# Second attention product with v as weights and the softmax moving, so that x comes out transposed

## The chip, the cores and the metric

One core of one Trainium2 chip. Times are device microseconds (us) of the whole program; lower is better. The kernel before takes 648.37 us (median of three runs, 646.69 to 648.68).

## What is computed

Chunked attention with 8 memory keys, then a SOLU layer with layer norm, then a mixture of 8 experts that sends each token to one expert. Only the first part is touched by the change:

```python
# q, k, v: (4, 8, 768, 64); mem_k, mem_v: (4, 8, 8, 64); chunk 32, left 16, right 8
for c in range(nc):                                  # 24 chunks of 32 queries
    k_full = concat([mem_k, k[:, :, l_start:r_end]]) # 8 + 56 keys
    v_full = concat([mem_v, v[:, :, l_start:r_end]])
    scores = q_c @ k_full.T / sqrt(64)
    a = exp(scores - max); a = a / (sum(a) + 1e-9)
    out[:, :, c_start:c_end] = a @ v_full            # the second attention product
x = out.transpose(0, 2, 1, 3).reshape(3072, 512)     # heads side by side
h = x @ w_in                                         # 512 -> 1024, then SOLU, layer norm, w_out
# ... then the experts
```

## The kernel before

The 3072 tokens go through in 24 row-tiles of 128 tokens, numbered i. A row-tile holds 4 chunks (`TC`) of 32 queries. Its 8 heads are 4 groups (`g`, `NG`) of 2 (`j`): j = 0 has its 64 keys on partitions 0 to 63, j = 1 on 64 to 127. `attention_steps` gives the steps of one row-tile (L352 to L458):

- `scores` (L357): 64 f32 matmuls of 64x32 weights into the PSUM tile `sc`.
- `row_max` to `normalise` (L372 to L405): the softmax, on VectorE, ScalarE and, for the last product, POOL.
- `transpose` (L407): four 128x128 transposes on PE into the PSUM tile `xb`, two banks, one buffer.
- `evacuate` (L414): ScalarE copies them to `aT` (keys on partitions, tokens along the row).
- `attend` (L419): the second product, 64 f32 matmuls. Weights are the softmax of one chunk and head (64 keys, 32 tokens), v moves (64 columns). Output: tokens on partitions, channels along the row, bank j.
- `x_hi`, `x_lo` (L433, L437): x times 256 as two f16 halves, the high one by ScalarE, the rest by VectorE (`low_half`, L185), into the tile `xhl` (two buffers). The profile puts `x_lo` at L186 with the names xhl<-xo.
- `x_turn` (L440): a transposing DMA from SP's queue turns `xhl` into `xT`, [channel, half and block of 128 channels, token], three buffers.

`product_in` of `solu_steps` (L526) takes `xT` as weights in 24 matmuls of 512 columns into the PSUM tile `h`, two banks and one buffer. `row_max`, `exp` and `times_h` (L543 to L559) read `h`; the next row-tile's product can only begin after `times_h`. Further down a row-tile comes `product_out` with w_out (24 matmuls, L607), `x2_hi`, `x2_lo`, `x2_turn`, and the routing.

The order on every engine is written out by hand. `at(t, fn)` notes a step with a planned time, and all of them are issued in order of t (L1363). From row-tile 7 on `steady(i)` gives the times (L460, `PERIOD` is 14.2); the first seven have tables (`STARTS`, `SOLU`, `CUTS`). An engine takes its instructions strictly in that order, so SP too: a DMA whose data isn't there holds up all DMAs behind it. SP issues the loads of q, k and v, of w_in and w_out (`load64`, L196), of the experts' weights, and the transposing DMAs of x, of the layer norm's output (`ln_turn`) and of x2.

In the first 70 us w_in and w_out, which come as 64-bit numbers, are turned into f16 halves by VectorE and ScalarE (`split64_steps`: L224, L229, L234, L241 and L186), beside the first row-tiles. `keep_warm` (L873) puts filling matmuls into PE's gaps there.

Near the end `other_slots` (L1088), in a branch that only runs when an expert gets far too many tokens, uses an `xhl` tile as scratch.

Of the kernel before, what the change touches and what calls it, by code (L numbers as in the profile page):

```python
# [8 lines left out]
F32 = mybir.dt.float32  # L9
F16 = mybir.dt.float16  # L10
# [9 lines left out]
P = 128  # L20
# [4 lines left out]
S_X = 2.0**8  # L25
# [13 lines left out]
def attention_solu_top1_moe(  # L39
# [145 lines left out]
    def low_half(lo, src, s, hi):  # L185
        nc.vector.scalar_tensor_tensor(out=lo, in0=src, scalar=s, in1=hi, op0=ALU.mult, op1=ALU.subtract)  # L186
# [165 lines left out]
    def attention_steps(i, s, a):  # L352

        u, tt, ib = i // 2, i % 2, i % TB
        v = {}

        def scores():  # L357
            qt, kt = QT[u], KT[u]
            sc = ps_s.tile([P, 2, HALF], F32, tag="s", name="sc")
            v["sc"] = sc[:, :, 0:NG * KW].rearrange("p j (g n) -> p j g n", g=NG)  # L360
            for g in range(NG):
                for c in range(TC):
                    for j in range(2):
                        nc.tensor.matmul(  # L364
                            out=v["sc"][CH * c:CH * (c + 1), j, g, :],
                            lhsT=qt[64 * j:64 * (j + 1), g, P * tt + CH * c:P * tt + CH * (c + 1)],
                            rhs=kt[64 * j:64 * (j + 1), g, TC * tt + c, :],
                            start=True,
                            stop=True,
                        )  # L370

        def row_max():  # L372
            if ib == 0:
                nc.vector.memset(v["sc"][0:CH, :, :, M:M + LEFT], MASKED)
            if ib == TB - 1:
                nc.vector.memset(v["sc"][P - CH:P, :, :, KW - RIGHT:KW], MASKED)
            v["mx"] = st.tile([P, 2, NG], F32, tag="mx", name="mx")
            nc.vector.tensor_reduce(out=v["mx"], in_=v["sc"], axis=AX.X, op=ALU.max)

        def shift():  # L380
            v["e"] = ap_.tile([P, NG, 2, KW], F32, tag="e", name="e")
            nc.vector.tensor_tensor(  # L382
                out=v["e"].rearrange("p g j n -> p j g n"),
                in0=v["sc"],
                in1=v["mx"].unsqueeze(3).to_broadcast([P, 2, NG, KW]),
                op=ALU.subtract,
            )

        def exp():
            nc.scalar.activation(out=v["e"], in_=v["e"], func=AF.Exp, scale=scale)  # L390

        def row_sum():
            v["sm"] = st.tile([P, NG, 2], F32, tag="sm", name="sm")
            nc.vector.tensor_reduce(out=v["sm"], in_=v["e"], axis=AX.X, op=ALU.add)

        def guard():
            nc.vector.tensor_scalar(out=v["sm"], in0=v["sm"], scalar1=1e-9, scalar2=None, op0=ALU.add)

        def recip():
            nc.vector.reciprocal(out=v["sm"], in_=v["sm"])  # L400

        def normalise():
            nc.gpsimd.tensor_tensor(  # L403
                out=v["e"], in0=v["e"], in1=v["sm"].unsqueeze(3).to_broadcast([P, NG, 2, KW]), op=ALU.mult
            )  # L405

        def transpose():  # L407

            v["xb"] = ps_x.tile([P, 2, HALF], F32, tag="x", name="xo")
            for g in range(NG):  # L410
                c = GD + g % 2 * P
                nc.tensor.transpose(v["xb"][:, g // 2, c:c + P], v["e"][:, g].rearrange("p j n -> p (j n)"), ident)

        def evacuate():  # L414
            v["aT"] = ap_.tile([P, NG, P], F32, tag="aT", name="aT")
            for z in range(2):
                nc.scalar.activation(out=flat(v["aT"][:, 2 * z:2 * z + 2]), in_=v["xb"][:, z, GD:GD + 2 * P], func=AF.Copy)

        def attend():  # L419
            aT, vv, xo = v["aT"], VW[u % 2], v["xb"]  # L420
            for g in range(NG):
                for c in range(TC):
                    for j in range(2):
                        nc.tensor.matmul(  # L424
                            out=xo[CH * c:CH * (c + 1), j, g * D:(g + 1) * D],
                            lhsT=aT[64 * j:64 * (j + 1), g, CH * c:CH * (c + 1)],
                            rhs=vv[64 * j:64 * (j + 1), TC * tt + c, g * D:(g + 1) * D],
                            start=True,
                            stop=True,
                        )  # L430
            v["xo"] = xo[:, :, 0:GD]

        def x_hi():  # L433
            v["xhl"] = lnp.tile([P, 2, 2, GD], F16, tag="xhl", name="xhl")
            nc.scalar.activation(out=v["xhl"][:, 0], in_=v["xo"], func=AF.Copy, scale=S_X)

        def x_lo():  # L437
            low_half(v["xhl"][:, 1], v["xo"], S_X, v["xhl"][:, 0])

        def x_turn():  # L440
            xT[i] = lnp.tile([P, 2 * KD, P], F16, tag="xT", name="xT", bufs=3)
            nc.sync.dma_start_transpose(out=xT[i], in_=v["xhl"].rearrange("p a j d -> p (a j d)"))

        steps = (row_max, shift, exp, row_sum, guard, recip, normalise)
        at(s[0], scores)
        if tt == 1 and u + 2 < NU and i > 3:
            if i > 5:
                at((i - 3) * PERIOD + 2.5, load_k, u + 2)
                at((i - 2) * PERIOD + 6.2, load_q, u + 2)
            at((i - 1) * PERIOD + 6.5, load_v, i + 3)  # L450
            at(i * PERIOD + 6.5, load_v, i + 4)
        for t, fn in zip(s[1:], steps):
            at(t, fn)
        for t, fn in zip(a, (transpose, evacuate, attend, x_hi, x_lo, x_turn)):
            at(t, fn)
        t = (i - 4) * PERIOD + 5.4
        at(WINDOWS.get(i, t), windows, i)
        at(MKEYS.get(i, t), memory_keys, i)  # L458
# [629 lines left out]
    def other_slots():  # L1088


        home = flat(lnp.tile([P, 2 * KD, P], F16, tag="x2T", name="x2T")).bitcast(F32)
        used = [0]

        def some_of(*shape):
            n = 1
            for x in shape:
                n *= x
            t, used[0] = home[:, used[0]:used[0] + n], used[0] + n
            return t.rearrange("p (a b) -> p a b", b=shape[1]) if len(shape) > 1 else t

        t1, cap, dl, be, em, es = (some_of(*x) for x in ((NT, E), (NT,), (NT,), (E,), (NO, E), (NO,)))
        oho = flat(lnp.tile([P, 2 * KD, P], F16, tag="x2T", name="x2T"))[:, 0:NT * NO].rearrange("p (a b) -> p a b", b=NO)
        keep_ = lnp.tile([P, 2, 2, GD], F16, tag="xhl", name="xhl").rearrange("p a j d -> p (a j d)").bitcast(F32)
        nc.vector.tensor_tensor(out=be, in0=rt["ends"], in1=rt["tr"], op=ALU.subtract)
        nc.vector.tensor_tensor(out=be, in0=be, in1=rt["room"][:, 2], op=ALU.subtract)
        for out_, of in ((cap, rt["room"][:, 0]), (dl, be)):
            nc.vector.tensor_tensor(out=t1, in0=oh_all, in1=of.unsqueeze(1).to_broadcast([P, NT, E]), op=ALU.mult)
            nc.vector.tensor_reduce(out=out_, in_=t1, axis=AX.X, op=ALU.add)
        nc.vector.tensor_tensor(out=cap, in0=rank_all, in1=cap, op=ALU.is_ge)
        nc.vector.tensor_tensor(out=dl, in0=rhi_all, in1=dl, op=ALU.add)  # L1110
        nc.vector.scalar_tensor_tensor(out=dl, in0=dl, scalar=1.0, in1=cap, op0=ALU.add, op1=ALU.mult)
        nc.vector.tensor_tensor(
            out=oho,
            in0=dl.unsqueeze(2).to_broadcast([P, NT, NO]),
            in1=iota_s[:, 1:NO + 1].unsqueeze(1).to_broadcast([P, NT, NO]),
            op=ALU.is_equal,
        )
        pt = ps_m.tile([P, 128], F32, tag="m", name="pm")
        ips = [pt[:, 0:NO], pt[:, 64:64 + NO]]
        for a in range(2):  # L1120
            three(ips[a], [(oav[:, i, a], oho[:, i]) for i in range(NT)])
        numbers("others", NO, ips, N - 1, keep_)
        nc.vector.tensor_tensor(
            out=em,
            in0=rt["ends"].unsqueeze(1).to_broadcast([P, NO, E]),
            in1=iota_s[:, 0:NO].unsqueeze(2).to_broadcast([P, NO, E]),
            op=ALU.is_le,
        )
        nc.vector.tensor_reduce(out=es, in_=em, axis=AX.X, op=ALU.add)
        nc.vector.tensor_scalar(out=rt["ctl"][:, 1, 0:NO], in0=es, scalar1=float(E - 1), scalar2=None, op0=ALU.min)  # L1130
# [367 lines left out]
```

## Time and profile before

| | |
|---|---|
| median of 3 runs | 648.37 us (646.69 to 648.68) |
| profiled execution | 647.3 us, span 645.6 us |
| mean granted PE clock | 0.987 |
| PE / VectorE / ScalarE / POOL busy | 607.8 / 419.3 / 299.1 / 176.5 us |
| DMA, all queues | 119.28 MB, mean 185 GB/s |

In the profile PE is TensorE's matmuls, PEld its weight loads, DVE VectorE, ACT ScalarE, POOL GpSimd and SP SyncE, which here only issues DMAs. L424 is line 424 of the kernel. Instructions are named output<-inputs: xo<-vw,aT is the second product. A matmul's recorded time includes its way through the array, so that many side by side overlap.

### The profile page before, as it was taken

The numbers are of one execution on the slowest core, as the hardware profiler recorded it, in microseconds if no ns is written. First come the engines' busy times: TensorE is split into PE (matmuls) and PEld (weight loads), VectorE is DVE, ScalarE is ACT, GpSimd is POOL, SyncE is SP. The second block draws the span as 40 slices with busy tenths as digits, with TensorE's granted clock in tenths as the row PEclk, the third lists the DMA queues.
The fourth block names the chain that finished last, engine by engine and source line by source line (L and its number), as shares of the span: only waits on it lengthen the run. The fifth ranks groups of instructions, "written<-read, shape, count | busy, mean of one in ns | idle before, by whom it ended". The sixth has DMA issues, their size and how long they took to land.

```text
span 645.6 us, 16935 instructions
## 1 busy us (share of the span) xinstructions
PE 607.8 (94%) x6919; PEld 333.3 (52%) x6919; DVE 419.3 (65%) x1216; ACT 299.1 (46%) x543; POOL 176.5 (27%) x201
## 2 busy tenths in 40 slices
PE   8787888999999999999999988999999999999993
PEld 4454344555545555555554443654554656657561
DVE  6999975878888788888786664447253435374020
ACT  5353644555556556565444223435243446354120
POOL 3122142323343324323334006022121313223101
PEclk9999898999999999999999989999999999999997
DMA  8899869989999999895539457988546576874201
GB/s 276 251 286 185 193 137 169 200 177 245 186 216 238 206 218 210 170 195 126 106 84 203 109 181 160 316 327 200 214 116 235 150 259 135 302 227 88 47 8 41
DMA packets 175654, 119.28 MB, mean 185 GB/s; under 512 B 133116, under 2 KB 157070, under 8 KB 175056
## 3 DMA queue, kind: packets, MB, share of 16 engines
q1 hardware_dynamic: 169488, 98.78, 64.7%
q0 software_dynamic: 6080, 19.34, 9.5%
q8 instruction: 56, 0.92, 0.6%
q14 instruction: 30, 0.25, 0.1%
HBM read 73.69 MB, written 12.94 MB: 134 GB/s over the span
## 4 chain that ended last, share of the span: by engine, by line
PE 31%; issue 26%; DVE 19%; DMA 11%; POOL 6%; ACT 5%; SPq 1%; POOLq 0%; ACTq 0%; DVEq 0%
PE pt L347 10%; PE h L535 10%; PE pg L347 5%; DMA out_dram<-eh,split 3%; POOL out_dram L1304 3%; POOL xg L1208 2%; DVE nm L545 2%; PE pt L1246 2%; DMA wd<-in_moe_w_in_dram 2%; ACT eh L553 2%; DVE eh L557 2%; PE xo L424 2%; DVE e L382 1%; PE sc L364 1%; DVE x L186 1%
## 5 line engine op out<-in xcount | busy, mean ns | idle before, releaser
L535 PE MATMUL h<-win_hl,xT 128*128 128x512 f16 x576 | 133.7, 383 | 6.2 <-DVE eh L557 1.9
L347 PE MATMUL pt<-wout_hl,lnT 128*128 128x512 f16 x552 | 129.5, 381 | 0.0
L1232 DVE SCALAR_TENSOR_TENSOR ru<-pg,ru 128x320 f16<-128x320 f32 (+5 forms) x72 | 37.7, 525 | 110.3 <-ACT ru L1231 110.3
L1246 PEld LDWEIGHTS <-ru 128*128 128x128 f16 (+2 forms) x1176 | 69.7, 100 | 62.2 <-issue 3.8
L535 PEld LDWEIGHTS <-xT 128*128 128x128 f16 x576 | 53.5, 98 | 67.5 <-issue 5.3
L347 PEld LDWEIGHTS <-lnT 128*128 128x128 f16 x576 | 53.6, 98 | 57.8 <-issue 1.4
L347 PE MATMUL pg<-xu,hl 128*128 128x320 f16 (+2 forms) x480 | 75.3, 317 | 2.6 <-DMA xu<-x 2.3
L1246 PE MATMUL pt<-hl,ru 128*128 128x512 f16 (+2 forms) x528 | 72.9, 321 | 0.0
L1231 ACT ACTIVATE ru<-pg 128x320 f16<-128x320 f32 (+5 forms) x72 | 33.5, 466 | 84.3 <-PE pg L347 83.2
L601 POOL TENSOR_TENSOR lnhl<-eh,lnhl 128x1024 f16<-128x1024 f32 x23 | 49.0, 2133 | 80.5 <-ACT lnhl L597 66.2
L347 PEld LDWEIGHTS <-hl 128*128 128x128 f16 x480 | 46.5, 99 | 27.9 <-DMA xu<-x 2.8
L1246 PE MATMUL pt<-wout_hl,ru 128*32 128x128 f16 (+2 forms) x648 | 59.9, 285 | 0.0
L347 PE MATMUL pg<-xu,win_hl 128*128 128x480 f16 (+3 forms) x384 | 59.3, 316 | 0.0
L1304 POOL DMA_INDIRECT out_dram<-eh,slots_sidx x17 | 17.6, 1037 | 144.3 <-ACT eh L1303 144.3
L347 PEld LDWEIGHTS <-win_hl 128*128 128x128 f16 x384 | 37.2, 98 | 21.3 <-issue 0.6
L553 ACT ACTIVATE eh<-h,nm 128x1024 f32<-128x1024 f32 x24 | 26.7, 1113 | 42.5 <-DVE zr L738 34.2
L186 DVE SCALAR_TENSOR_TENSOR hl<-wf,hl 128x1024 f16<-128x1024 f32 x32 | 38.6, 1223 | 6.4 <-ACT hl L1195 6.0
L403 POOL TENSOR_TENSOR e<-e,sm 128x512 f32<-128x512 f32 x24 | 26.7, 1114 | 49.3 <-ACT win_hl L241 20.2
L586 POOL TENSOR_TENSOR rt<-vr,mhalf 128x1 f32<-128x1 f32 x24 | 15.2, 633 | 79.1 <-DVE vr L582 79.0
L1195 ACT ACTIVATE hl<-wf 128x1024 f16<-128x1024 f32 x32 | 32.9, 1047 | 2.8 <-DMA wf<-in_moe_w_dram 2.8
L574 ACT ACTIVATE junk<-eh,su 128x1024 f16<-128x1024 f32 x24 | 27.5, 1148 | 13.9 <-DVE pr L569 9.8
L557 DVE SCALAR_TENSOR_TENSOR eh<-h,eh 128x1024 f32<-128x1024 f32 x24 | 29.3, 1221 | 4.9 <-ACT eh L553 4.8
(186 smaller groups left out, 825.3 us busy)
## 6 DMA issues: line engine op xcount, KB each, us to landing
wf<-in_moe_w_dram SPq DMA_DIRECT2D x14, 2048.0 KB
vw<-in_v_dram SPq DMA_DIRECT2D x96, 112.0 KB
kr<-in_k_dram SPq DMA_DIRECT2D x12, 560.0 KB
qt<-in_q_dram SPq DMA_DIRECT2D x12, 512.0 KB
x2d<-x POOLq DMA_DIRECT2D x23, 260.0 KB, 3.7
wd<-in_moe_w_in_dram SPq DMA_DIRECT2D x4, 1024.0 KB
wd<-in_moe_w_out_dram SPq DMA_DIRECT2D x4, 1024.0 KB
wf<-in_moe_w_dram SPq DMA_DIRECT2D x8, 512.0 KB
```

Of the source, the lines that this page charges most:

```text
L186: nc.vector.scalar_tensor_tensor(out=lo, in0=src, scalar=s, in1=hi, op0=ALU.mult, op1=ALU.subtract)
L347: nc.tensor.matmul(out=out_ap, lhsT=a, rhs=b_, start=(z == 0), stop=(z == n - 1))
L535: nc.tensor.matmul(out=v["h"][:, n * HALF:(n + 1) * HALF], lhsT=xt[:, a * KD + kk], rhs=win_hl[:, b_, kk, n * HALF:(n + 1) * HALF], start= ...
L553: nc.scalar.activation(out=v["e"], in_=v["h"], func=AF.Exp, bias=v["nm"], scale=IH, accum_out=v["se"])
L557: nc.vector.scalar_tensor_tensor(out=e, in0=v["h"], scalar=IH, in1=e, op0=ALU.mult, op1=ALU.mult, accum_out=v["su"])
L574: nc.scalar.activation(out=junk, in_=v["e"], func=AF.Square, bias=v["su"], scale=1.0, accum_out=v["sq"])
L601: eng.tensor_tensor(out=v["ln"][:, 1], in0=v["e"], in1=v["ln"][:, 0], op=ALU.subtract)
L1195: nc.scalar.activation(out=hl[b, m][:, 0, cs], in_=wf[m if of is None else of][:, cs], func=AF.Copy, scale=(S_W1, S_W2)[m])
L1231: nc.scalar.activation(out=r[:, 0, f, 0:cap(n)], in_=ps, func=AF.Relu)
L1232: nc.vector.scalar_tensor_tensor(out=r[:, 1, f, 0:cap(n)], in0=ps, scalar=0.0, in1=r[:, 0, f, 0:cap(n)], op0=ALU.max, op1=ALU.subtract)
L1246: nc.tensor.matmul(out=y_t[n, piece][q * m:(q + 1) * m, 0:DM // fold], lhsT=r[:, a, kk, at_:at_ + m], rhs=wt[:, b_, kk, q * DM // fold:(q ...
L1304: put = nc.gpsimd.indirect_dma_start(out=out if fold == 1 else out.rearrange("n (h d) -> (n h) d", h=fold), out_offset=bass.IndirectOffset ...
```

## The change

In `attend` the two operands trade places: the weights are v of one chunk and head (64 keys, 64 channels), and the softmax moves (32 tokens). The output has channels on partitions and tokens along the row: head h of a pair of groups g2 takes partitions 64h to 64h + 63, and bank j stays. With that `x_hi` and `x_lo` write `xT` itself, and `x_turn` and its DMA are taken out; `xT` is allocated in `x_hi`. The loops are turned so that matmuls in a row go to the four combinations of h and j. `xhl` is left with one buffer for the scratch of `other_slots`.

```diff
         def attend():
             aT, vv, xo = v["aT"], VW[u % 2], v["xb"]
-            for g in range(NG):
+            for g2 in range(NG // 2):
                 for c in range(TC):
-                    for j in range(2):
-                        nc.tensor.matmul(
-                            out=xo[CH * c:CH * (c + 1), j, g * D:(g + 1) * D],
-                            lhsT=aT[64 * j:64 * (j + 1), g, CH * c:CH * (c + 1)],
-                            rhs=vv[64 * j:64 * (j + 1), TC * tt + c, g * D:(g + 1) * D],
-                            start=True,
-                            stop=True,
-                        )
+                    t0_ = g2 * P + CH * c
+                    for h in range(2):
+                        g = 2 * g2 + h
+                        for j in range(2):
+                            nc.tensor.matmul(
+                                out=xo[D * h:D * (h + 1), j, t0_:t0_ + CH],
+                                lhsT=vv[64 * j:64 * (j + 1), TC * tt + c, g * D:(g + 1) * D],
+                                rhs=aT[64 * j:64 * (j + 1), g, CH * c:CH * (c + 1)],
+                                start=True,
+                                stop=True,
+                            )
             v["xo"] = xo[:, :, 0:GD]
 
         def x_hi():
-            v["xhl"] = lnp.tile([P, 2, 2, GD], F16, tag="xhl", name="xhl")
-            nc.scalar.activation(out=v["xhl"][:, 0], in_=v["xo"], func=AF.Copy, scale=S_X)
+            xT[i] = lnp.tile([P, 2 * KD, P], F16, tag="xT", name="xT", bufs=3)
+            v["xT"] = xT[i].rearrange("p (a j k) t -> p a j (k t)", a=2, j=2)
+            nc.scalar.activation(out=v["xT"][:, 0], in_=v["xo"], func=AF.Copy, scale=S_X)
 
         def x_lo():
-            low_half(v["xhl"][:, 1], v["xo"], S_X, v["xhl"][:, 0])
-
-        def x_turn():
-            xT[i] = lnp.tile([P, 2 * KD, P], F16, tag="xT", name="xT", bufs=3)
-            nc.sync.dma_start_transpose(out=xT[i], in_=v["xhl"].rearrange("p a j d -> p (a j d)"))
+            low_half(v["xT"][:, 1], v["xo"], S_X, v["xT"][:, 0])
...
-        for t, fn in zip(a, (transpose, evacuate, attend, x_hi, x_lo, x_turn)):
+        for t, fn in zip(a, (transpose, evacuate, attend, x_hi, x_lo)):
             at(t, fn)
...
-        keep_ = lnp.tile([P, 2, 2, GD], F16, tag="xhl", name="xhl").rearrange("p a j d -> p (a j d)").bitcast(F32)
+        keep_ = lnp.tile([P, 2, 2, GD], F16, tag="xhl", name="xhl", bufs=1).rearrange("p a j d -> p (a j d)").bitcast(F32)
```

## Rows read from the trace of the kernel before

**Rows 1.** The page: PE's busy share in 40 slices of the span, in tenths.
```profile
PE 607.8 (94%) x6919; PEld 333.3 (52%) x6919; DVE 419.3 (65%) x1216; ACT 299.1 (46%) x543; POOL 176.5 (27%) x201
...
PE   8787888999999999999999988999999999999993
```
**Rows 2.** Busy time by stretches (us): PE, PEld, DVE, ACT, POOL, clock, DMA share, GB/s.
```profile
20.00:68.60 48.60, 37.57 (x676) 21.17 (x675) 46.72 (x74) 21.64 (x39) 12.82 (x8) 1.00 0.87 228
...
100.00:340.00 240.00, 238.55 (x3482) 123.72 (x3463) 197.74 (x729) 134.24 (x271) 78.55 (x96) 0.99 0.88 182
```
**Rows 3.** PE's waits, 0 to 102 us: who waited for whom, total, times, longest.
```profile
PE h L535 <- DVE eh L557: 1.9, 1, 1.9
PE h L535 <- DMA xT<-xhl: 1.7, 1, 1.7
PE h L535 <- DVE win_hl L186: 1.4, 1, 1.4
```
**Rows 4.** PE's waits, 102 to 340 us.
```profile
PE xo L424 <- ACT aT L417: 0.3, 1, 0.3
PE sc L364 <- issue: 0.3, 1, 0.3
```
**Rows 5.** The chain of waits in order of time: start, us, what.
```profile
49.78 5.40 DMA wd<-in_moe_w_out_dram
...
68.69 6.95 PE h L535 x24
```
**Rows 6.** L224, 50 to 57 us: records' min/median/max (ns); timelines of VectorE and POOL.
```profile
L224 DVE TENSOR_SCALAR da<-wd x3: 684/1316/1317, 49.7 to 55.2; 128x1024 int32<-128x1024 int32 x3
...
53.75 2.77 DVE L224 TENSOR_SCALAR da<-wd 128x1024 int32<-128x1024 int32 x2
...
53.47 2.49 POOL L403 TENSOR_TENSOR e<-e,sm 128x512 f32<-128x512 f32 x2 [4.79 <-DVE su L566]
```
**Rows 7.** SP's timeline and its waits; tile xT: the turns' records, who waited.
```profile
49.78 0.58 SPq L203 DMA_DIRECT2D wd<-in_moe_w_out_dram  x1
...
SPq L442 <- DVE e L382: 8.8, 1, 8.8
...
L442 SPq DMA_TRANSPOSE xT<-xhl x24: 1231/1242/2407, 22.8 to 331.6; - x24
...
  PEld L535: 4.1, 3
```
**Rows 8.** PE's timeline in the steady stretch: start, us, what.
```profile
157.11 0.86 PE L424 MATMUL xo<-vw,aT 64*32 64x64 f32 x64
...
158.78 0.45 PE L347 MATMUL pm<-wg_hl,x2T 128*128 128x16 f16 x12
159.09 2.32 PE L535 MATMUL h<-win_hl,xT 128*128 128x512 f16 x10
```
**Rows 9.** Matmuls and weight loads by shape: records' min/median/max, or busy and mean.
```profile
L424 PE MATMUL xo<-vw,aT x1536: 212/217/313, 18.3 to 328.3; 64*32 64x64 f32 x192
...
L412 PE MATMUL xo<-ident,e x96: 272/273/329, 16.9 to 326.6; 128*128 128x128 f32 x96
...
L347 PEld LDWEIGHTS <-x2T x288: 94/96/98, 91.9 to 379.1; 128*128 128x128 f16 x144
...
L1246 PEld LDWEIGHTS <-ru 128*64 128x64 f16 x288 | 15.3, 110 | 2.5 <-issue 2.5
...
L1246 PEld LDWEIGHTS <-ru 128*32 128x32 f16 x384 | 5.4, 97 | 1.2 <-issue 1.2
```
**Rows 10.** x_hi in tile xhl's records: min/median/max (ns).
```profile
L435 ACT ACTIVATE xhl<-xo x24: 573/576/597, 19.3 to 330.3; 128x512 f16<-128x512 f32 x24
```
**Rows 11.** L424 alone, by stretches: length, PE busy (matmuls), PEld, clock, DMA, GB/s.
```profile
157.11:157.36 0.25, 0.25 (x32) 0.25 (x33) 1.00 1.51 441
...
99.69:100.06 0.37, 0.37 (x31) 0.37 (x33) 0.50 1.52 164
99.69:100.57 0.88, 0.88 (x64) 0.88 (x64) 0.50 1.28 205
```

## The prediction

> **What bounds the kernel now.** I read the busy line and the slices first [rows 1]: TensorE has work for 94% of the span, and its slices stand at 9 almost everywhere but in the first seven (some 113 us). So the question for every edit is whether it shortens TensorE's own queue, or one of the few places where that queue stands still. The table by stretches [rows 2] shows where these are. From 100 to 340 us, with attention and SOLU side by side, PE is busy for 238.55 of 240 us. From 20 to 68.6 us PE has gaps (37.57 of 48.60 us) and VectorE next to none (46.72). The list of PE's waits says the same from the other side: from 102 to 340 us two waits of 0.3 us are all that it lists [rows 4], and before that VectorE, on `times_h` or the halves of w_in, stands beside one wait of 1.7 us on the DMA of xT [rows 3]. The chain of waits [rows 5] crosses from VectorE to PE at 68.69 us, when the third row-tile's `times_h` frees the bank of h. From there on it mostly follows PE. An edit is thus worth something if it moves that crossing, or if it shortens PE's work after it.
>
> **The change part by part.**
> *The 24 transposing DMAs.* SP issues each in about 1.24 us [rows 7], 24 x 1.242 = 29.8 us of SP's queue, and the DMA engines lose their packets. In steady state neither is on the path: attention's x is ready well before its reader (`attend` is planned at (i-2) x PERIOD + 11, `product_in` at i x PERIOD), and PE lists no DMA wait from 102 to 340 us [rows 4]. I count nothing there. The cover is that distance, some 17 planned us, which the shorter way only lengthens.
>
> In the first 68 us the issue also held up whatever stood behind it on SP: for the third tile SP stood 8.8 us for x_lo, and the load of the last w_out quarter followed the turn at 49.78 [rows 7] and is the 5.40 us step of the chain [rows 5]. Without the turn the load can go that much earlier, as soon as its buffer is free. What is late next is VectorE itself: it did L224 of another quarter first, and the two together took 2.77 us, records of 1.316 and 1.317 where one alone has 0.684 [rows 6], so that 2.77 - 2 x 1.317 = 0.13 us was idle. Their excess lies beside two normalising operations on POOL (2.49 us from 53.47, until 55.96); no DMA is in it. So -0.1 us. The bounds: below, all VectorE idle time from 20 to 68.6 us, 48.60 - 46.72 = 1.9 us [rows 2]; above, the loads now crowd what they overtake, for which I allow 0.5. Other loads that were held behind the turns of tiles 0 and 1 feed the windows and scores, and VectorE, whose order is fixed, comes to these no sooner.
>
> PE's 1.7 us wait on xT (and the 4.1 of its weight loads) [rows 3, 7] is before the crossing too. The product that waits there next needs halves of w_in that VectorE is still splitting (the 1.4 us on win_hl in rows 3), so I count it at nothing; if that cover is gone it is inside the 1.9.
>
> *x_hi and x_lo.* Same shapes and engines, 0.58 us for x_hi [rows 10]; only the place written differs. They take xT's buffer (three deep) at x_hi instead of after x_lo. Its reader is the product of three tiles before, planned 26 us before x_hi, so ACT, in whose order the next row-tile's work stands behind x_hi, gains no wait. Nothing. The one allocation of xhl that is left belongs to a branch for overflowing experts, with no row in this trace: nothing.
>
> *The product itself.* 64 weight loads and 64 matmuls a tile before and after. A matmul now has 64 columns of v as weights and moves 32 instead of 64. Today 8 array tiles (two row halves, four column quarters) work side by side, then 4 (two halves, two halves). Stream time: a 128-column f32 matmul is recorded at 273 ns and a 64-column one at 217, so 64 columns are 56 ns [rows 9]. Shared by 8 tiles that is 7.0 ns a matmul; 32 columns are 28 ns, shared by 4 tiles 7.0 as well. No gain from the stream, but a shorter last one: 28 ns.
>
> The weight load doubles: f16 loads of 64 and 32 columns are recorded at 110 and 97 ns [rows 9], 13 ns for 32, so 27 ns for 64, no longer well under the stream of its tile but level with it. No row shows such a pair. Bounds: if the load stays under the stream, 7.0 ns a matmul. The nearest row where the load is the longer part is L347's logits, 12 matmuls of 16 columns from 158.78 to 159.09, 0.31/12 = 26 ns each [rows 8]. Its load is recorded at 96 ns and a 64-column one at 110 [rows 9], so 40 ns a tile, 10 a matmul over four.
>
> How much of that counts depends on what limits the product today. From its first to its last start it takes 0.86 - 0.22 = 0.64 us [rows 8, 9]. In the table for L424 alone [rows 11] the first 32 matmuls begin within 0.25 us, and the other 32 need the remaining 0.39. At the half clock (PEclk 0.50, the product at 99.69) the first 31 need 0.37 of 0.88 us and the rest 0.51, less apart. So at the full clock the array is not what holds the second half; the instructions come later than the array could take them, and their number stays. I charge the longer load to the first half alone: 32 x (0 to 3.0 ns) = 0 to 0.10 us, and take 0.05, the middle, since neither row is nearer. With the shorter last stream 0.05 - 0.028 = +0.02 us a tile. Products after the crossing without a longer wait behind them: tiles 6 to 23, 18 of them: +0.4 us, with bounds of 18 x -0.028 = -0.5 and 18 x 0.07 = +1.3.
>
> By the Trainium skill, "TensorE: Matmul & The Clock Gate", section "Packing small matmuls: row/col tiling", a weight load runs beside matmuls in flight only where its row group differs. By this rule the load would add to the stream of its own tile. The trace doesn't agree for today's shape: 32 matmuls in 0.25 us are under 8 ns each, where load and stream in turn would need (13 + 56)/8 = 8.6.
>
> *Sum.* -0.1 + 0.4 = +0.3 us. The profiled execution took 647.3 us (span 645.6 and 1.7 around it), within the three runs (646.69 to 648.68) and 1.07 under their median; I put the sum on the mean of the three, 647.9, which gives 648.2.
>
> **Rivals.**
> *The product gets longer (slower).* A 64x64 tile is held by one pair as long as a 64x32 tile is today, 53 to 56 ns, either because load and stream take turns (27 + 28) or because 32 columns take no less than 64. Four tiles then give 55/4 = 14 ns a matmul, 64 x 14 = 0.90 us for 0.64, less 0.03: +0.23 us on 18 tiles, +4.1, so 652.0. It decides once a pair holds its tile for more than about 40 ns (10 a matmul, today's mean). For it: no fp32 pair with a load as long as its stream is in the trace, and four tiles hide less than eight. Against it: in the first half of today's product loads are hidden. Chance 0.24; in its worst form the two column halves also share one load path (40 ns for each of 32 loads, 1.28 us, +11 us).
> By the Trainium skill, "TensorEngine Tiling (Array Packing)", section "Instruction Overhead", a matmul has an overhead of about 60 cycles, so that one column costs what 60 do, and no tiling factor should be taken from a small dimension. The logits' 26 ns agree (60 cycles at 2.4 GHz are 25); whether it holds for each pass of a 32-column f32 matmul no run here shows.
>
> *The start gets shorter (faster).* The SP queue without its turns lets the crossing at 68.69 come earlier by VectorE's whole idle time, -1.9 us, 646.0, and more if POOL and VectorE then meet less often. For it: SP held for 8.8 us by one turn [rows 7]. Against it: VectorE's 0.13 us. Chance 0.12.
>
> *The product gets shorter (faster).* The second half runs at the pace of the first, 64 x 7 = 0.45 us: -0.19 - 0.03 on 18 tiles, -4.0, 643.9. Against it: the same number of instructions. Chance 0.08.
>
> **How the numbers follow.** The forecast has 0.54, the slower rival 0.24 with 0.02 for other losses, the faster ones 0.20. The likeliest case alone spans 646.4 to 649.7 (its terms together from -1.5, with half of the start's idle time, to +1.8). The range reaches into the slower rival, 645.4 to 652.4. A measurement of this kernel can't tell 0.3% (1.9 us of 648.37) from no change, so: faster 0.20, within 0.54, slower 0.26.
>
> **What would show it.** The x64 group of the product at 0.82 to 0.90 us in PE's timeline (0.86 now), its matmul at about 190 ns (217); 1.0 or more would be the slower rival, 0.65 the faster. PE's step to h L535 in the chain still near 68.6 us, with no DMA of w_out in front of VectorE; a crossing before 67 would prove my reading of the start wrong. The wait of PE on the DMA of xT gone from the list, and a wait on VectorE in its place. The distance from one row-tile's product to the next in the steady stretch unchanged to 0.05 us.

## The result, and the profile after

The kernel after takes 652.0 us (median of 8 runs, 650.83 to 654.99), the kernel before beside it 648.58 (8 runs, 646.69 to 652.16): a ratio of 1.0058 [1.0029, 1.0086]. It is slower by 3.4 us. The profiled execution of after took 651.16 us, its span 649.4, at a mean clock of 0.988.

From the page of after: busy times, PE's slices and the DMA queues (packets, MB, share).

```profile
PE 613.3 (94%) x6919; PEld 342.1 (53%) x6919; DVE 417.2 (64%) x1216; ACT 301.0 (46%) x543; POOL 175.5 (27%) x201
...
PE   7897879999999999999999988989999999999993
...
q1 hardware_dynamic: 144144, 92.48, 56.5%
```

PE has as many instructions as in [rows 1], but is busy 5.5 us longer, and its weight loads 8.8 us. VectorE has 2.1 us less.

The product (now L427): its records by shape, then PE's timeline around row-tile 7, which answers to [rows 8].

```profile
L427 PEld LDWEIGHTS xo<-aT,vw x1536: 128/135/228, 17.8 to 332.6; 64*64 64x64 f32 x192
L427 PE MATMUL xo<-aT,vw x1536: 211/219/313, 17.8 to 332.6; 64*64 64x32 f32 x192
```
```profile
119.51 1.14 PE L427 MATMUL xo<-aT,vw 64*64 64x32 f32 x64
120.58 1.04 PE L347 MATMUL pt<-wout_hl,lnT 128*128 128x512 f16 x4
...
124.00 0.86 PE L364 MATMUL sc<-kt,qt 64*32 64x64 f32 x64
```

The product's group lasts 1.14 us and not 0.86, so 1.14 - 0.22 = 0.92 us from its first to its last start (0.64 before), 14.6 ns for each of 63 steps. Most of the difference lies in the first half. The first 32 matmuls begin within 0.25 us in [rows 11] and the others need 0.39; after, the same view of L427 has 0.45, and 0.47 are left for the others.

```profile
119.51:119.96 0.45, 0.45 (x32) 0.45 (x32) 1.00 1.11 394
```

The matmul's record has not become shorter (219 ns against 217 in [rows 9]), though half as many columns move.

The steady stretch, from row-tile 7's product to row-tile 23's, in the table by stretches (length, PE busy, PEld, DVE, ACT, POOL, clock, DMA share, GB/s): before, then after.

```profile
118.26:327.66 209.40, 207.95 (x3107) 108.11 (x3106) 175.06 (x639) 120.69 (x244) 70.15 (x88) 1.00 0.92 190
```
```profile
119.51:331.71 212.20, 211.99 (x3108) 113.55 (x3107) 174.28 (x639) 122.63 (x244) 70.16 (x88) 1.00 0.74 169
```

Here is most of the loss: the same work takes 212.20 - 209.40 = 2.80 us longer. PE is busy 4.04 us longer. The sixteen products of the stretch add up to 10.42 us from first to last starts before and to 15.05 after, 4.63 more, and PE's idle time falls from 1.45 to 0.21 us. Where that idle time stood is shown by PE's groups from 118 to 332 us (the last two numbers are the idle time in front of the group, and the part of it that the profile names), before and then after.

```profile
L424 PE MATMUL xo<-vw,aT 64*32 64x64 f32 x1088 | 14.7, 224 | 1.2 <-ACT aT L417 0.3
L364 PE MATMUL sc<-kt,qt 64*32 64x64 f32 x1024 | 14.0, 224 | 0.3 <-issue 0.3
```
```profile
L427 PE MATMUL xo<-aT,vw 64*64 64x32 f32 x1044 | 19.1, 220 | 0.2 <-ACT aT L417 0.2
```

DMA's share falls from 0.92 to 0.74, and the time doesn't follow it.

PE's waits of after, 0 to 102 us and 102 to 340 us, the answer to [rows 3, 4].

```profile
PE xo L412 <- DVE xT L186: 3.7, 2, 1.9
PE h L535 <- DVE eh L557: 3.1, 3, 1.7
...
PE h L535 <- DVE win_hl L186: 1.4, 1, 1.4
```
```profile
PE xo L427 <- ACT aT L417: 0.2, 1, 0.2
```

The wait on the transposing DMA of xT is gone. All five traces of the kernel before have it (1.3 to 2.3 us), none of the three of after. What took its place can't be read from the lists: the wait on `times_h` is 3.1 us here and 1.9 before, but over all traces it is 1.9 to 3.4 before and 2.1 to 3.1 after. The longest wait, of the transposes on x_lo, is as long as it was; [rows 3] leaves it out:

```profile
PE xo L412 <- DVE xhl L186: 4.0, 2, 2.1
```

The chain of waits at the start, the answer to [rows 5]:

```profile
46.22 1.11 PE xo L427 x64
47.33 0.02 issue
47.35 0.61 ACT xT L439
47.95 0.02 issue
47.98 0.69 DVE xT L186
...
54.12 2.69 DVE da L224 x2
...
70.28 5.30 DVE wout_hl L186 x8
```

Before, the chain went into the load of a w_out quarter for 5.40 us. Now that load is early (SP issues w_out's quarters by 34 us), and VectorE's own work stands there, row-tile 2's product in front of it. The step that the prediction calls the crossing, the start of row-tile 3's input product, comes at 68.99 us, 68.69 before. In this trace the chain doesn't go over to PE there: it stays on VectorE, from 70.28 us with the halves of w_out, until 85.26 us. Three of the five traces of before do the same, the two others of before and the two later ones of after go over to PE as in [rows 5]: here VectorE and PE are about level.

One more place: row-tile 6's product, at PE's half clock after a wait, 0.88 us in [rows 11], as after has it:

```profile
99.81 1.93 PE L427 MATMUL xo<-aT,vw 64*64 64x32 f32 x64 [0.75 <-ACT aT L417]
```

From first to last start that is 1.64 us at a granted clock of 0.50, 0.77 more than the 0.87 before.

### The profile page after: what moved, and what is told of

The parts are those of the page before. It is cut to its first block, busy times and chain, and to the rows that moved or that the text cites. A ratio compares the mean times of both kernels' runs of the same rounds, so it can differ in the third digit from the quotient of the medians.

```text
span 649.4 us, 16820 instructions
## 1 busy us (share of the span) xinstructions
PE 613.3 (94%) x6919; PEld 342.1 (53%) x6919; DVE 417.2 (64%) x1216; ACT 301.0 (46%) x543; POOL 175.5 (27%) x201
## 4 chain that ended last, share of the span: by engine, by line
PE 76%; DVE 10%; DMA 7%; issue 2%; ACT 2%; POOL 1%; SPq 0%; POOLq 0%; ACTq 0%; DVEq 0%
PE pg L347 17%; PE pt L1246 17%; PE pt L347 17%; PE h L535 16%; PE xo L427 4%; PE sc L364 2%; DMA wd<-in_moe_w_in_dram 2%; DMA wf<-in_moe_w_dram 2%; DVE wout_hl L186 2%; PE xo L412 1%; PE pm L347 1%; DVE da L234 1%; DVE da L229 1%; DMA x<-x2d,slots_gidx 1%; DMA kr<-in_k_dram 1%
## 5 line engine op out<-in xcount | busy, mean ns | idle before, releaser
L535 PE MATMUL h<-win_hl,xT 128*128 128x512 f16 x576 | 132.1, 379 | 4.5 <-DVE eh L557 3.1
L535 PEld LDWEIGHTS <-xT 128*128 128x128 f16 x576 | 53.2, 98 | 64.3 <-issue 4.2
L347 PE MATMUL pg<-xu,hl 128*128 128x320 f16 (+2 forms) x480 | 73.6, 312 | 1.7 <-DMA xu<-x 1.7
L427 PEld LDWEIGHTS xo<-aT,vw 64*64 64x64 f32 x1536 | 26.1, 139 | 13.0 <-ACT aT L417 11.7
```

The source lines that it names most:

```text
L347: nc.tensor.matmul(out=out_ap, lhsT=a, rhs=b_, start=(z == 0), stop=(z == n - 1))
L427: nc.tensor.matmul(out=xo[D * h:D * (h + 1), j, t0_:t0_ + CH], lhsT=vv[64 * j:64 * (j + 1), TC * tt + c, g * D:(g + 1) * D], rhs=aT[64 * j ...
L535: nc.tensor.matmul(out=v["h"][:, n * HALF:(n + 1) * HALF], lhsT=xt[:, a * KD + kk], rhs=win_hl[:, b_, kk, n * HALF:(n + 1) * HALF], start= ...
```

## The experiments

The theory to be tested: a weight load of 64 f32 columns takes some 53 ns, twice what I had taken from f16 records, and holds the tile for that time, while the shorter stream runs beneath it ("load"). The rivals are the two reasons that the prediction gave for its slower case: load and stream take turns on a tile ("turns"), or 32 columns cost what 64 do ("floor"). Beside these stands what the DMAs are worth.

**Pairs by themselves.** Behind the end of the changed kernel come loops of one shape each, on one array tile and then spread over four or eight, with 12 warm-up matmuls between them. In f32 each call shows as two pairs of load and matmul.

```diff
+    def pair(r, c, n, s, src):
+        nc.tensor.matmul(
+            out=banks[r][c * 32:c * 32 + n, 0:s], lhsT=src[64 * r:64 * r + 64, 0:n], rhs=src[64 * r:64 * r + 64, 0:s], start=True, stop=True
+        )
...
+    for _ in range(32):
+        pair(0, 0, 64, 32, ident)
...
```

> The changed kernel with series of test matmuls behind its end, after filling matmuls that keep the clock up; read is the distance from one pair (weight load and matmul) to the next, first on one array tile, then on all. Theory 'load': an f32 load takes 0.83 ns a column (53 ns for 64) with the stream hidden beneath it, and a pair holds its tile for the longer of the two plus about 5 ns. Rival 'turns': the load takes 0.41 ns a column and load and stream take turns. Rival 'floor': a pair holds its tile about 58 ns whatever is in it. One tile, f32, load x stream columns: 64x32 load 58, turns 58, floor 58. 64x64: load 58 to 61, turns 86, floor 58 to 61. 64x128: load 110, turns 137, floor 110. 32x32: load 32, turns 44, floor 58. 32x64: load 56, turns 72, floor 58. One tile, f16, 64x32: load 32 to 40, turns 43, floor 58 if it knows no type. Over all tiles: f32 64x32 on four tiles 14.6 ns a matmul under all three; f16 on four tiles 8 to 10, turns 11; f32 32x32 on eight tiles 6.6 to 10 (then set by how fast instructions come), 32x64 on eight 7 to 10.

PE's timeline of that run: start, length of the group, tile, moving shape, count.

```profile
660.82 4.21 PE L1457 MATMUL pt<-ident 64*64 64x32 f32 x64
...
668.33 3.94 PE L1457 MATMUL pt<-ident 64*64 64x64 f32 x64
...
674.26 7.20 PE L1457 MATMUL pt<-ident 64*64 64x128 f32 x64
...
683.45 2.21 PE L1457 MATMUL pt<-ident 64*32 64x32 f32 x64
...
687.64 3.76 PE L1457 MATMUL pt<-ident 64*32 64x64 f32 x64
...
693.38 1.18 PE L1457 MATMUL pt<-wide 64*64 64x32 f16 x32
...
696.55 0.68 PE L1457 MATMUL pt<-wide 64*64 64x32 f16 x64
...
699.22 2.07 PE L1457 MATMUL pt<-ident 64*64 64x32 f32 x128
...
703.28 1.52 PE L1457 MATMUL pt<-ident 64*32 64x32 f32 x157
...
706.82 1.04 PE L1457 MATMUL pt<-ident 64*32 64x32 f32 x99 [2.02 <-issue]
...
709.85 1.79 PE L1457 MATMUL pt<-ident 64*32 64x64 f32 x128
```

A group less its last record (some 0.2 us), through the steps in it, gives the time per pair. On one tile, f32: 64 weights and 64 moving columns 59 ns, 64 and 128 110 ns, 32 and 32 32 ns, 32 and 64 56 ns; in f16 64 and 32 take 32 ns. For 64 and 32 in f32 the sum gives 63 ns, but there the granted clock fell before the group's end (0.50 from 664.4 us); the median from start to start is 58 ns. So doubling the stream under 64 weights costs nothing, half the weights under 32 columns take little more than half the time, and so does f16. "Turns" falls, since it put 64 and 64 at 86 and 64 and 128 at 137; "floor" falls, since 32 and 32 are down at 32. The rows fit a pair that holds its tile for the longer of load and stream: 32 more weights add 26 ns where the load is the longer (32 to 58), 64 more columns add 54 where the stream is (56 to 110). Over four tiles the f32 pair of the new product takes (2.07 - 0.22)/127 = 14.6 ns, a quarter of 58 and the very pace in the kernel. Over eight tiles the old product's pair, 32 weights and 64 columns, was expected at 7 to 10 ns and takes 12.4: one of the 127 steps is 321 ns long, and the others come at 10.0 on average, near the pace of the product in the kernel before (0.64/63 = 10.2 ns).

By the Trainium skill, "TensorE: Matmul & The Clock Gate", section "LDWEIGHTS (loading the stationary operand)", a load takes its columns divided by 1.2, in ns: 53 for 64 and 27 for 32. The f32 rows agree (58 and 32, each 5 ns more); the f16 row does not (32 for 64 columns). The Trainium skill's same page, section "Packing small matmuls: row/col tiling", in one sentence lets a load run beside matmuls of another row group only, and in another also where it goes to a background weight buffer. The first doesn't hold for these rows: 64 and 64 on one single tile take 59 ns, where the load of the Trainium skill and the stream in turn would be 53 + 56 = 109 (an estimate). Which buffer a load went to, no row shows.

**A wide stream in the kernel.** The product moves 64 columns where after moves 32; the next step overwrites the 32 that are too many.

```diff
+                    n_ = CH if (g2, c) == (NG // 2 - 1, TC - 1) else 2 * CH
...
-                                out=xo[D * h:D * (h + 1), j, t0_:t0_ + CH],
+                                out=xo[D * h:D * (h + 1), j, t0_:t0_ + n_],
...
-                                rhs=aT[64 * j:64 * (j + 1), g, CH * c:CH * (c + 1)],
+                                rhs=flat(aT)[64 * j:64 * (j + 1), g * P + CH * c:g * P + CH * c + n_],
```

> The changed kernel with 64 columns moving in each matmul of the second product instead of 32 (the second half is the next chunk's, overwritten by the next matmul); loads and their number stay, 4 of 64 matmuls stay at 32. 'Load': the stream of 56 ns still fits beside a load of 53, so a round of four stays at 58 to 62 ns, the product at 0.92 to 0.99 us, and the time within +1.5 us of the changed kernel, 1.004 to 1.008 of the one before. 'Turns': 27 + 56 + 3 = 86 ns a round, 1.38 us a product, +0.46 on 17 row-tiles, +8 us, 1.018 of before. 'Floor': like load.

PE's timeline at row-tile 7:

```profile
120.80 1.14 PE L428 MATMUL xo<-aT,vw 64*64 64x64 f32 x64
```

Four of the 32 calls, eight of the 64 pairs, stay at 32 columns. The group takes 1.14 us, to the hundredth what it is with half the columns. The whole is 1.0070 [1.0042, 1.0098] of before (after: 1.0058), row-tile 7 to 23 takes 212.24 us (212.20). In the kernel as in the table the stream lies beneath the load.

**The turns put back.** The new product, and beside it the 24 transposing DMAs as before, from xT into a tile that nobody reads.

```diff
+        def x_turn():
+            spare = lnp.tile([P, 2, 2, GD], F16, tag="xhl", name="xhl").rearrange("p a j d -> p (a j d)")
+            nc.sync.dma_start_transpose(out=spare.rearrange("p (k t) -> p k t", t=P), in_=flat(xT[i]))
...
```

> The changed kernel with the 24 transposing DMAs put back at their old place on SP's queue, from xT into a tile that nobody reads. If the DMAs and SP's time are off the path: the time of the changed kernel, 652 us, ratio to the kernel before 1.004 to 1.008. If taking them away had given something back (rival: the start, 1 to 2 us, or relief of the full DMA engines later on): slower than the changed kernel by that much, 653 to 655, ratio 1.008 to 1.011.

The ratio is 1.0071 [1.0042, 1.0101], against 1.0058 [1.0029, 1.0086] without them. The stretch, again by the table:

```profile
120.11:331.87 211.76, 211.76 (x3107) 113.28 (x3106) 174.35 (x639) 122.46 (x244) 70.17 (x88) 1.00 0.92 189
```

The DMA share is back at 0.92 and the stretch not longer. By the whole the two expected cases can't be told apart, since both lie in the interval; the stretch shows no relief from the removed DMAs. What they give is below what these runs can tell.

**The change in two halves.** First only row-tiles 0 to 6 get the new product and lose the turn (`TURNED = range(0, 7)`), then only 7 to 23.

```diff
+            if i in TURNED:
...
+            else:
+                for g in range(NG):
+                    for c in range(TC):
...
+    TURNED = range(0, 7)
```

> The new product and no turn for row-tiles 0 to 6 alone; from 7 on the old product with its turn. If the loss lies in the steady stretch (17 longer products on PE's queue) and the start neither gains nor loses: 648.6 us, ratio 0.998 to 1.002. If the start gains from SP's freed queue: below 0.997. Rival: part of the loss is the start's, where the trace after the change shows row-tile 7 late by 1.2 us, of which 0.8 is row-tile 6's product at the half clock: then 649.5 to 650, ratio 1.001 to 1.003.

> The other part of the cut: old product and turn for row-tiles 0 to 6, new product and no turn from 7 on. The traces so far put 2.8 us on the stretch from row-tile 7's product to row-tile 23's (209.4 us before, 212.2 after, 209.6 with the first seven alone). If that loss is the product's and the rest of the loss is the start's: 209.4 + 2.8 in this stretch, row-tile 7's product near 118.3 as before, time +2.8, ratio 1.003 to 1.006. If the steady part is the whole loss: ratio as the changed kernel, 1.006, with 3.8.

The first seven alone: 1.0027 [0.9998, 1.0055], the rest alone: 1.0040 [1.0016, 1.0064]; together 1.0067, beside 1.0058 for the whole change. The first is not clear of no change; its middle lies where the rival had it, with part of the loss in the start. The second fits both of its cases. Row-tile 7's product, expected near 118.3 us there, began at 121.67, after a crossing at 71.28. The stretch from row-tile 7 to 23 of the two:

```profile
120.90:330.48 209.58, 207.90 (x3107) 108.03 (x3106) 175.74 (x639) 121.12 (x244) 70.14 (x88) 1.00 0.90 190
```
```profile
121.67:333.68 212.01, 212.01 (x3107) 113.50 (x3107) 174.38 (x639) 122.77 (x244) 70.22 (x88) 1.00 0.74 169
```

The loss of that stretch comes and goes with the product in it. Where only the first seven have the change, it stands at 209.58 with 1.68 us of idle PE, as before.

**Quarters.** Each product on 32 of the 64 channels, as weights of 32 columns on eight tiles: half the load and the same stream, but 128 pairs a row-tile.

```diff
-                    for h in range(2):
-                        g = 2 * g2 + h
+                    for h in range(4):
+                        g = 2 * g2 + h // 2
...
-                                lhsT=vv[64 * j:64 * (j + 1), TC * tt + c, g * D:(g + 1) * D],
+                                lhsT=vv[64 * j:64 * (j + 1), TC * tt + c, g * D + h % 2 * CH:g * D + h % 2 * CH + CH],
```

> The changed kernel with each product step cut in two halves of 32 channels: twice as many loads of 32 columns and twice as many matmuls of 32, over eight array tiles. By the load alone it should be shorter than the changed product: 128 pairs x 32/8 ns = 0.51 us. The pair table gave 8.3 ns a pair for this mixture, set by how fast instructions come to the array: then 128 x 8.3 = 1.06 us, longer than the changed kernel's 0.92, and some 2.5 us later at the end.

It took 688.07 us in its one run, some 36 more than the changed kernel where 2.5 were expected. The product itself is 1.10 us from first to last start, 8.6 ns a pair, the pace of eight tiles in the table ((1.52 - 0.19)/156 = 8.5 ns). The rest is elsewhere. PE's waits from 125 to 345 us and its timeline at one of them:

```profile
PE pm L347 <- issue: 6.7, 3, 2.4
PE h L535 <- issue: 4.2, 3, 2.1
PE sc L364 <- issue: 3.1, 3, 1.5
PE h L535 <- DVE eh L593: 2.2, 1, 2.2
```
```profile
262.08 0.37 PE L347 MATMUL pm<-wg_hl,x2T 128*128 128x16 f16 x9
264.66 0.25 PE L347 MATMUL pm<-wg_hl,x2T 128*128 128x16 f16 x3 [2.20 <-issue]
264.76 3.48 PE L535 MATMUL h<-win_hl,xT 128*128 128x512 f16 x8
```

PE stands still and the profile names nothing that holds it, and the eight matmuls behind it take 3.48 us where ten take 2.32 in [rows 8]; the granted clock is 0.52 from 264.70 to 268.20 us. From row-tile 7 to 23 it needs 239.73 us, with 239.73 - 221.56 = 18.2 us of idle PE. The queue that brings instructions moves more, here by the page of quarters and then by that of after:

```profile
q8 instruction: 68, 1.11, 0.7%
```
```profile
q8 instruction: 56, 0.92, 0.6%
```

In the window of that stall (261 to 266 us) two of its packets go. The series of 256 short pairs in the table has such a stall too (2.02 us at 706.82), and so, shorter, has the kernel before (0.75 us in row-tile 0's product, in its second trace). That PE waits for instructions is the reading that fits; no run here isolates it.

**Both kernels again, for the stages.** One trace of each can't tell 0.3 us at the crossing from chance, so each was run again unchanged.

> The kernel before, unchanged, for a second profile of its start. In the first one no product or score of row-tiles 0 to 3 stood still in its middle, and the crossing to row-tile 3's input product was at 68.69 us; in the four profiles with the new product it was at 68.99 to 70.51 and one or two such stalls of 0.5 to 2.8 us lay before it, with fetches of instructions by DMA near them. If these stalls come with the change (rival), this profile has none and the crossing is at 68.7 within 0.2. If they come and go between executions: a stall over 0.4 us before 40 us, and a crossing later than 69.

> The changed kernel, unchanged, for a second profile of its start. The part of the start that the change itself explains is the longer product of row-tile 2, which lies on the chain to VectorE: crossing at 68.69 + 0.3 = 69.0 if no stall reaches the chain, up to 70.5 if one does. The stretch from row-tile 7's product to row-tile 23's at 212.2 within 0.3 whatever the start does.

They took 650.3 us (before) and 656.92 (after), one run each; 17 runs of the kernel before beside them have a median of 652.36. Now the crossing comes at 70.33 us before and at 68.70 after (69.0 to 70.5 expected), the other way round than in the first two traces: the 0.3 us are not the change's. A stall of 0.75 us lies before 40 us in this trace of before, so such stalls come and go between executions. A question came up beside it: all kernels with the change, in whole or in part, had PE wait for VectorE at `ru`, when the experts begin, near 423 us.

> The kernel before, unchanged, for one more trace. In the traces so far PE waits on VectorE (tile ru, some 423 us) for 0 and 0.7 us in the kernel before and for 1.9 to 3.4 us in all six with the change or a part of it, also where only the first seven row-tiles have it. Theory 'belongs to the change': 0 to 1.0 us here. Rival 'differs from execution to execution': 1.5 us or more in at least one of the three traces of the kernel before taken now. Both: row-tile 7's product to 23's 209.3 to 209.6 us, row-tile 6's product 0.87 us.

> The same kernel before and the same two theories: 0 to 1.0 us on ru where the wait belongs to the change; 1.5 us or more in at least one of the three where it doesn't.

> The same kernel before and the same two theories: 0 to 1.0 us on ru where the wait belongs to the change; 1.5 us or more in at least one of the three where it doesn't.

> The kernel after, unchanged, for a third trace. Where the wait on ru belongs to the change: 1.9 us or more; where it differs between executions it may be anything from 0 to 3.5. Both: row-tile 7's product to 23's 211.8 to 212.4 us, the product 0.92 us, row-tile 6's 1.64 us.

They took 651.98, 648.35 and 653.02 us (before) and 655.85 (after). PE's waits from 405 to 460 us in the third and fifth trace of before and the third of after:

```profile
PE pg L347 <- DMA xu<-x: 3.6, 1, 3.6
PE pt L1246 <- DVE ru L1232: 0.6, 1, 0.6
```
```profile
PE pg L347 <- DMA xu<-x: 3.9, 1, 3.9
```
```profile
PE pt L1246 <- DVE ru L1232: 2.4, 2, 1.7
PE pg L347 <- DMA xu<-x: 1.1, 1, 1.1
```

The wait on `ru` goes with the change: 0 to 0.7 us in five traces of before, 1.9 to 3.4 in seven with the change or a part. By what way, also where only the first seven row-tiles have it, no run shows. It costs nothing that shows: from row-tile 23's product to the end both kernels spread alike (last column; from first starts in PE's timeline, lowest to highest).

| traces | crossing, us | crossing to row-tile 7 | 7 to 23 | 23 to the end |
|---|---|---|---|---|
| before, 5 | 68.7 to 70.3 | 49.2 to 50.4 | 209.27 to 209.40 | 317.9 to 321.7 |
| after, 3 | 68.7 to 71.3 | 50.5 to 52.2 | 212.20 to 212.38 | 317.7 to 321.8 |

The third stage is the one that repeats to 0.2 us and differs by 2.8 to 3.1. The second lies higher by 0.1 to 3.0 us, 1.5 between the middle traces; the products of row-tiles 5 and 6 explain 0.27 + 0.77 = 1.0 of it (row-tile 6's is 0.87 us in all five traces of before, 1.64 in all three of after). The other experiments narrow this stage: 50.2 to 51.7 us in four more traces with the new product in it, 50.4 in the one with the old, so that the medians of seven and six are 50.5 and 49.8. With the 2.8 of the third the two products make 3.8 us, and the medians of the whole differ by 3.4.

## Why the prediction was wrong

It said 648.2 us and no change; the change costs 3.4 us. The 652.0 lie within the stated range only because its upper end, 652.4, was put there for the slower rival; the likeliest case by itself ended at 649.7.

- **The failing step** is the weight load in "The product itself". "The weight load doubles: f16 loads of 64 and 32 columns are recorded at 110 and 97 ns [rows 9], 13 ns for 32, so 27 ns for 64, no longer well under the stream of its tile but level with it." The product is f32, and its load runs at half the pace of an f16 one: a pair with 32 weights held a tile for 32 ns, one with 64 for 58, where f16 needs 32 for 64. The bound that I set from it, 10 ns a matmul, was too low as well: 14.6. So the term of the sum for the product, +0.02 us on each of 18 row-tiles, was +0.27. A row of the kernel before could have warned me: the product's own load of 32 f32 columns is recorded at 106 ns there, 9 above the f16 load of 32 columns (97), nearly what another 32 f16 columns cost (110).

```profile
L424 PEld LDWEIGHTS xo<-vw,aT x1536: 102/106/175, 18.3 to 328.3; 64*32 64x32 f32 x192
```

- **"I charge the longer load to the first half alone"** was right for the greater part: the first 32 pairs begin within 0.45 us and no longer 0.25, the others need 0.47 and no longer 0.39. Of the 0.28 us by this view, 0.20 lie in the first half, and at 14.6 ns a pair the tiles hold the second too.
- **The stretch** gave back 1.2 us: 16 products are 4.6 us longer, and PE's idle time goes from 1.45 to 0.21. Before, PE stood in front of some products (1.2 us ahead of L424; after, 0.2 ahead of L427) and once in front of the scores (0.3). One of these waits, of 0.3 us, is put down to `evacuate`; the others are too short to be listed, and that they are the same is likely, not shown. The prediction had no such term. The 0.6 us that are left between 4.6 - 1.2 and the measured 2.8 are not accounted for.
- **Row-tile 6** was counted like the other seventeen, though [rows 11] showed its product at the half clock: 0.77 us and not 0.27.
- **The slower rival** had the size: 55 ns a tile, 14 ns a matmul, 0.90 us, 652.0 in all; measured are 58, 14.6, 0.92 and 652.0. That the last agrees to the tenth is luck: 4.1 us on 647.9 there, 3.4 on 648.58 here, with the idle time that was given back. Both its reasons were wrong: load and stream do not take turns, and 32 columns do not cost what 64 do. I held it for less likely since loads are hidden in today's first half; they are there, since in the table 32 weights alone hold a tile for 32 ns and with 64 moving columns for 56.
- **The DMAs** were read rightly. Putting them back changed nothing that can be measured, the wait on xT went, and the w_out load left the chain without the crossing moving beyond its own spread. That there would be "no DMA of w_out in front of VectorE" came true. That a wait on VectorE would stand in the place of the one on xT is not shown: the waits on `times_h` of both kernels spread alike.
- **The faster rivals** had nothing for them: the product is not at the pace of the first half, nor does the start get shorter.
- **What I said would show it** mostly did: "1.0 or more would be the slower rival" (1.14), and the matmul's record at 219 instead of 190. That record didn't shrink with its stream; in the table it goes with the longer of load and stream (192 ns for 32 weights and 32 columns, 216 to 219 for 32 and 64, 64 and 32, 64 and 64, and 269 for 64 and 128). From one product to the next it is 2.80/16 = 0.18 us longer in the steady stretch, where I had "unchanged to 0.05 us". The chain's step to h L535 is there at 68.70 us in the second trace of after and at 71.34 in the third; in the first the chain takes VectorE's way.

## What to carry to other kernels

Before two operands trade places, work out for each tile of the array the longer of weight load and stream, in the data type that runs, and divide by the number of tiles: here 56/8 = 7.0 became 58/4 = 14.5. After, the product runs at that pace (14.6); before, it didn't reach it (10.2), so look as well for what the pairs come at when the tiles are free. Fewer columns in motion are no gain where the weights grow by as much. DMAs that the bounding engine hardly waits for, here 24 of them with 6.3 MB, pay for no longer instruction on that engine.

## What the runs showed of the hardware

- One f32 matmul call is two pairs of load and matmul in the trace (32 calls a row-tile, 64 pairs); the prediction's "64 matmuls" are these pairs.
- Load and stream of one single tile overlap: 64 weights with 32 or 64 moving columns hold it for 58 to 59 ns, with 128 for 110.
- Spread over eight tiles, pairs of 32 and 32 columns come at 8.5 ns, twice the 32/8 = 4 that the tiles would allow; f16 pairs on four tiles at (0.68 - 0.18)/63 = 7.9, which is 32/4, so they don't tell. Something other than the tiles holds the short f32 pairs at 8.5 ns, no run shows what, and neither 128 short pairs nor the 64 of the kernel before (10.2 ns) reach the tiles' pace.
- 64 pairs more in a row-tile took 1.10 us in place of 0.92, and 18 us of PE idle time came with them, most of it without a named releaser.
